# Batch 0's v pieces issued by ScalarE, small constants by SyncE, and a later gate for the first weight load

## The chip, the core and the metric

The kernel runs on one core of a Trainium2 chip. The core has a matrix engine (TensorE, PE in the profile), a vector engine (VectorE, DVE), an engine for activation functions (ScalarE, ACT), a general engine (GpSimd, POOL) and SyncE (SP), which here only issues DMAs. Sixteen DMA engines move the data. SyncE, ScalarE and GpSimd each have a DMA queue of their own. The metric is the device time of one execution in microseconds, and lower is better.

## What is computed

The reference is linear attention without a softmax, then an RMS norm per head, then a gated convolutional feed-forward block. Inputs are float32: q, k, v of 8 batches x 8 heads x 576 positions x 64, w_in 512 x 1024, conv_w 3 x 1024, w_out 1024 x 512.

```python
kv  = einsum('bhsd,bhse->bhde', k, v)            # 64 x 64 per head
o   = einsum('bhsd,bhde->bhse', q, kv)
o   = o / sqrt(mean(o * o, axis=-1) + 1e-6) * g_norm
x   = o.transpose(0, 2, 1, 3).reshape(8, 576, 512)
h   = maximum(x @ w_in, 0)
c   = sum over 3 taps of conv_w[tap] * h shifted by tap - 1 along the sequence
out = (h * sigmoid(c)) @ w_out                   # 8 x 576 x 512
```

## The kernel before, in words

The whole program is one list, `ORDER` (lines 59 to 122). Each word of it names a small function and its arguments; a number behind an @ chooses a buffer or PSUM bank. The words are run from left to right, and at the end each instruction is tied to the one before it on its engine, so every engine works through its instructions in exactly the order of the list. An engine that waits holds back everything that stands behind it.

Heads are put in pairs: 128 partitions hold two heads of 64, so each of q, k and v of a batch is four column blocks (t = 0 to 3). Positions are kept as 64 partitions x 9 rows. Batches 1 to 7 are loaded by GpSimd, which turns float32 into bfloat16 on the way (`Lq`, `Lk`, `Lv`, line 321). So are the weights: `Li` (line 335) brings w_in in two halves, `Lo` (line 339) w_out. Batch 0 goes another way. `pre` (lines 226 to 250) has SyncE load it as float32 in twelve pieces, in the order of `HEAD` (line 218): q.t.s is two blocks and part of the columns (256 KB for q.0.0 and q.1.0, 320 KB for q.0.1 and q.1.1), k.t and v.t are one block each (288 KB). `cad` casts a piece to bfloat16 on VectorE (line 358), `caa` on ScalarE (line 360).

The small constants (three rows of convolution taps and the norm's weights, `cw_rows`) are loaded by ScalarE (lines 237 and 238). `ct` (line 268) transposes them on TensorE; `pc` (lines 274 to 281) has VectorE copy them out of PSUM and rescale them, in eight small instructions.

The part of the list that counts here is its head. On TensorE it is: `fi.78.64`, 78 matmuls on zeros whose results nobody reads; `ct`; `qt.0.0.0`, transposes of q; `fi.17.512`, 17 more matmuls on zeros; `kv.0.0.1`, the k-v products of the first four heads; then `fi.1`, `qt`, `ot`, `fi.3`, `oq`, `fi.8` and `kv.0.1.1`, the products of the other four heads. These `fi` words keep TensorE busy at the start (line 263). On VectorE it is: cast of q.0.0, `pl` (memsets), `pc`, casts of k.0, v.1, q.1.0 and k.2, `ps` (lines 300 to 305), cast of v.3, `qd` (line 417), `dg.7`, `kvd.0.1.1` (line 388), `dg.4`, cast of q.0.1 and so on. On ScalarE: casts of v.0 and k.1, `qa`, `kva`, `sq`, casts of v.2 and k.3, `nl`. The head ends with `hp` (line 555), the first matmuls with w_in; from there on it is mostly long runs of matmuls.

`gt` (line 352) is the gate of the weight load. It copies one column of a staged piece on GpSimd, and since GpSimd works in order, w_in and all later loads of that queue are issued only when that piece has arrived. Here the piece is q.1.0.

DMAs issued by SyncE and ScalarE report their arrival on eight semaphores, which the framework gives out in rotation over both engines. A DMA that gets a semaphore whose earlier user has not yet arrived waits for it before it is issued. In this kernel the ninth to fourteenth of the loads, k.2, v.2, k.3, v.3, q.0.1 and q.1.1, have such waits, on the constants' taps, q.0.0, the norm's weights, k.0, v.0 and k.1.

Of the kernel before, what the change touches and what calls it, by code (L numbers as in the profile page):

```python
# [56 lines left out]


ORDER = """
pre@0,1 af gt.q.1.0 Li.0.4 fi.78.64@0 ct@0 cad.q.0.0@0 caa.v.0.0@0 pl pc cad.k.0.0@0 caa.k.1.0 cad.v.1.0 cad.q.1.0  # L60
cad.k.2.0 ps cad.v.3.0 qt.0.0.0@2 fi.17.512@1 qa.0.0.0@0 kv.0.0.1@4 kva.0.0.1@0 fi.1.512@0 qt.0.1.0@6 qd.0.1.0@1
Li.4.4 ot.0.0.0@2 sq.0.0.0@0 dg.7 fi.3.512@0 oq.0.0.0@4 fi.8.512@0 caa.v.2.0 caa.k.3.0 kv.0.1.1@0 fi.2.512@6 kvd.0.1.1
ot.0.1.0@6 fi.2.512@0 dg.4 nl.0.0.0@0 sq.0.1.0@1 cad.q.0.1 qt.0.0.1@4 qa.0.0.1 mo.0.0.0@0 cad.q.1.1 oq.0.1.0@0
# [62 lines left out]
def kernel(  # L126
# [11 lines left out]
    nc = tc.nc  # L138
    B, H, S, D = q.shape
    D_model = H * D  # L140
    D_ff = moe_w_in.shape[1]
    P = 128
# [5 lines left out]
    NF = D_ff // P  # L148
# [11 lines left out]
    def ring(r, shape, dtype, name):  # L160
        return work.tile(shape, dtype, name=name, tag=f"{r}{slots.pop(0)}", bufs=1)


    def half(i):
        return slice(i * D, (i + 1) * D)
# [4 lines left out]
    def heads(x, b, t0, n):  # L170
        return src[x][b, 2 * t0:2 * (t0 + n)].rearrange("(t i) (p r) d -> (i p) t (r d)", i=2, r=R)

    T = {}
# [7 lines left out]
    NR = 3 * NF + 1  # L181
# [3 lines left out]
    cw_rows = consts.tile([NR, P], FP32, name="cw_rows")  # L185
    cw = consts.tile([P, NR], FP32, name="cw")
# [24 lines left out]
    def act_table(which):  # L211
        if act_set[0] != which:
            act_set[0] = which
            nc.scalar.preload_act_table_set(  # L214
                {"rs": "abs_reciprocal_sqrt_and_small", "sig": "sigmoid_and_others"}[which])

    RS = ((0, 4), (4, 9))
    HEAD = "q.0.0 k.0.0 v.0.0 k.1.0 v.1.0 q.1.0 k.2.0 v.2.0 k.3.0 v.3.0 q.0.1 q.1.1"

    def cols(b, s):  # L220
        if b == 0:
            return tuple(r * D for r in RS[s])
        return s * HS, (s + 1) * HS

    @op
    def pre():
        T["stg"] = ring("h", [P, 2, NT, R * D], FP32, "stg")
        T["stq"] = ring("h", [P, NT, R * D], FP32, "stq")
        for what in HEAD.split():
            x, t, s = what.split(".")  # L230
            t, s = int(t), int(s)
            if x == "q":
                ts, (c0, c1) = slice(2 * t, 2 * t + 2), cols(0, s)
                nc.sync.dma_start(out=T["stq"][:, ts, c0:c1], in_=heads("q", 0, 2 * t, 2)[:, :, c0:c1])
            else:
                nc.sync.dma_start(out=T["stg"][:, "kv".index(x), t:t + 1, :], in_=heads(x, 0, t, 1))  # L236
        nc.scalar.dma_start(out=cw_rows[:3 * NF, :], in_=moe_conv_w.rearrange("k (f p) -> (k f) p", p=P))
        nc.scalar.dma_start(
            out=cw_rows[NR - 1:NR, :].rearrange("o (i d) -> o i d", i=2),
            in_=g_norm.unsqueeze(0).unsqueeze(1).to_broadcast([1, 2, D]))  # L240
        act_table("rs")
        nc.vector.memset(zero, 0.0)  # L242
        nc.vector.memset(ident, 0.0)
        nc.vector.memset(ones, 0.0)
        for i in range(2):
            nc.vector.memset(ones[half(i), half(i)], 1.0)
        nc.vector.memset(eps_sb, eps)
        for t in taps:
            nc.vector.memset(t[:, 0, :, :, 7:8], 0.0)
            nc.vector.memset(t[:, 1, :, :, S:S + 1], 0.0)  # L250
# [425 lines left out]
    for token in ORDER.split():  # L676
        what, _, at = token.partition("@")
# [44 lines left out]
```

## Time and profile before

| | |
|---|---|
| median of 3 runs | 187.1 us (186.58 to 187.44) |
| the profiled execution | 186.68 us, of which the span from first to last instruction is 184.9 us |
| TensorE busy | 174.6 us, 94% of the span |
| VectorE, ScalarE, GpSimd busy | 145.7, 147.9 and 19.2 us |
| first matmul with w_in (line 555) | 19.73 us after the start |

Times in the rows are microseconds from the start of the span. In a timeline row stand the start, the length, the engine, the line, the operation, what it writes and reads, and, in square brackets, how long the engine sat idle before it and what ended that. An engine name with a q (SPq, ACTq, POOLq) is an instruction that issues a DMA; its length is the issuing alone, and the data arrive later. The chain of waits is followed backwards from the last instruction, at each step to what released it.

### The profile page before, as it was taken

How to read it: one execution, taken by the hardware profiler on the slowest of the kernel's cores; microseconds unless marked ns; L12 is line 12 of the kernel's file. 1: busy time of each engine (PE TensorE's matmuls, PEld its weight loads, DVE VectorE, ACT ScalarE, POOL GpSimd, SP SyncE). 2: the span in 40 equal slices, each digit the busy share in tenths (PEclk: the TensorE clock that was granted, in tenths of full speed). 3: DMA queues.
4: the chain of work that ended last, by engine and by line, in shares of the span. 5: the costliest groups of instructions: out<-in, count | busy, mean ns of one | idle time of the engine just before them, and what ended most of it. 6: DMA issues, size and time to landing. Idle time of an engine off the chain costs nothing.

```text
span 184.9 us, 5517 instructions
## 1 busy us (share of the span) xinstructions
PE 174.6 (94%) x2358; PEld 107.5 (58%) x2358; DVE 145.7 (79%) x283; ACT 147.9 (80%) x232; POOL 19.2 (10%) x30
## 2 busy tenths in 40 slices
PE   7998899999989899999999999999999999999990
PEld 7543677645657587447567784454578754444450
DVE  3578701864589979999599999997999999999650
ACT  2456789877788999999999997999979977673830
POOL 1095200300413001600000000000000000000000
PEclk9999999999999999999999999999999999999997
DMA  5999999999999996899940000102320001417294
GB/s 176 289 345 200 206 210 205 209 208 255 231 208 208 208 209 103 131 208 221 278 97 4 4 0 4 57 20 97 130 100 0 0 0 57 174 51 289 80 380 167
DMA packets 20816, 27.82 MB, mean 150 GB/s; under 512 B 1184, under 2 KB 15288, under 8 KB 20792
## 3 DMA queue, kind: packets, MB, share of 16 engines
q0 software_dynamic: 13184, 14.48, 46.7%
q1 hardware_dynamic: 7568, 12.98, 20.0%
q8 instruction: 18, 0.29, 0.6%
q14 instruction: 6, 0.05, 0.1%
q10 hardware_dynamic: 40, 0.01, 0.0%
HBM read 32.52 MB, written 9.44 MB: 227 GB/s over the span
## 4 chain that ended last, share of the span: by engine, by line
PE 73%; DVE 13%; DMA 4%; ACT 3%; issue 2%; SPq 2%; DVEq 0%; ACTq 0%
PE banks L629 30%; PE banks L540 24%; PE banks L555 4%; DMA stg<-in_v_dram 4%; PE banks L605 3%; DVE qT L417 3%; PE banks L434 2%; PE banks L376 2%; PE banks L407 2%; SPq L236 2%; DVE x L526 2%; DVE h L619 1%; DVE taps L579 1%; ACT rs L472 1%; DVE taps L578 1%
## 5 line engine op out<-in xcount | busy, mean ns | idle before, releaser
L629 PE MATMUL banks<-w_out_sb,h 128*128 128x512 bf16 x280 | 64.2, 380 | 0.3 <-DVE row L640 0.3
L540 PE MATMUL banks<-x,w_in_sb 128*128 128x288 bf16 x448 | 57.6, 286 | 0.7 <-DVE x L526 0.2
L540 PEld LDWEIGHTS <-w_in_sb 128*128 128x128 bf16 x448 | 43.2, 98 | 13.6 <-issue 1.6
L629 PEld LDWEIGHTS <-h 128*128 128x128 bf16 x280 | 26.3, 98 | 31.3 <-issue 2.5
L595 ACT ACTIVATE taps<-taps,cw 128x576 bf16<-128x576 bf16 (+1 forms) x40 | 37.3, 967 | 7.8 <-DVE taps L589 7.8
L546 ACT ACTIVATE h<-banks 128x576 bf16<-128x576 f32 x56 | 34.2, 658 | 2.7 <-PE banks L540 2.7
L619 DVE TENSOR_TENSOR h<-h,taps 128x1152 bf16<-128x1152 bf16 (+1 forms) x24 | 22.8, 953 | 11.8 <-ACT taps L612 10.1
L442 ACT ACTIVATE sq<-banks 128x576 bf16<-128x576 f32 (+2 forms) x32 | 20.4, 660 | 4.4 <-PE banks L434 4.1
L584 DVE TENSOR_TENSOR taps<-taps 128x1152 bf16<-128x1152 bf16 (+1 forms) x20 | 20.0, 999 | 0.4
L589 DVE TENSOR_TENSOR taps<-taps,h 128x1152 bf16<-128x1152 bf16 (+1 forms) x20 | 19.8, 996 | 0.5
L578 DVE TENSOR_SCALAR taps<-h,cw 128x576 bf16<-128x576 bf16 (+1 forms) x40 | 17.2, 429 | 1.1 <-ACT h L546 1.1
L579 DVE TENSOR_SCALAR taps<-h,cw 128x576 bf16<-128x576 bf16 (+1 forms) x40 | 17.4, 436 | 0.0
L635 ACT ACTIVATE row<-banks 128x512 f32<-128x512 f32 x26 | 14.9, 600 | 2.9 <-PE banks L629 2.5
L483 DVE SCALAR_TENSOR_TENSOR x<-banks,cw,rs 128x576 bf16<-128x576 f32 (+2 forms) x16 | 12.9, 814 | 4.9 <-ACT rs L472 4.8
L263 PE MATMUL banks<-zero 128*128 128x64 bf16 (+1 forms) x113 | 12.9, 282 | 1.2 <-DVE zero L242 1.2
L526 DVE SCALAR_TENSOR_TENSOR x<-o,cw,banks 128x576 bf16<-128x576 f32 x16 | 12.2, 810 | 2.1 <-PE banks L520 2.1
L472 ACT ACTIVATE rs<-banks,eps_sb 128x576 f32<-128x576 f32 (+2 forms) x16 | 11.6, 738 | 1.2 <-PE banks L455 1.1
L417 DVE COPY qT<-banks 128x1152 bf16<-128x1152 bf16 (+2 forms) x15 | 10.4, 712 | 2.3 <-PE banks L407 1.5
L214 ACT ACT_TABLE_LOAD x8 | 10.3, 1283 | 2.3 <-issue 2.2
L448 ACT ACTIVATE o<-banks 128x576 f32<-128x576 f32 x16 | 10.4, 675 | 0.3 <-PE banks L434 0.3
L321 POOL DMA_DIRECT2D k_sb<-in_k_dram x7 | 5.3, 755 | 45.0 <-PE banks L376 44.4
L434 PE MATMUL banks<-qT,kvb 64*64 64x288 bf16 (+2 forms) x128 | 8.6, 296 | 1.3 <-DVE qT L417 0.9
(78 smaller groups left out, 143.1 us busy)
## 6 DMA issues: line engine op xcount, KB each, us to landing
out_dram<-row SPq DMA_DIRECT2D x35, 256.0 KB, 2.4
q_sb<-in_q_dram POOLq DMA_DIRECT2D x7, 576.0 KB, 17.9
k_sb<-in_k_dram POOLq DMA_DIRECT2D x7, 576.0 KB, 13.6
v_sb<-in_v_dram POOLq DMA_DIRECT2D x7, 576.0 KB, 15.6
stg<-in_k_dram SPq DMA_DIRECT2D x4, 288.0 KB, 4.0
stg<-in_v_dram SPq DMA_DIRECT2D x4, 288.0 KB, 6.4
w_in_sb<-in_moe_w_in_dram POOLq DMA_DIRECT2D x2, 512.0 KB, 8.6
w_out_sb<-in_moe_w_out_dram POOLq DMA_DIRECT2D x1, 1024.0 KB, 20.0
```

What stands on the lines that cost most here:

```text
L417: nc.vector.tensor_copy(to, fr)
L442: nc.scalar.activation(T["sq", b, u, s], T["o", b, u, s], AX.Square)
L526: nc.vector.scalar_tensor_tensor(x_part(b, u, s), T["o32", b, u, s], g_sb, T["sp", b, u, s], op0=AL.mult, op1=AL.mult)
L540: nc.tensor.matmul(ps[:, s, :c1 - c0], w_in_sb[:, t, f * P:(f + 1) * P], T["x", b][:, t, c0:c1], start=(t == 0), stop=(t == NT - 1))
L546: nc.scalar.activation(h_of(b, f), T["hm", b, f][:, :, :HS].rearrange("p e (r n) -> p e n r", r=R), AX.Relu)
L578: nc.vector.tensor_scalar_mul(tap[:, 0, f % 2, :n, 8:8 + S], h[:, f], cw[:, f:f + 1])
L579: nc.vector.tensor_scalar_mul(tap[:, 1, f % 2, :n, :S], h[:, f], cw[:, 2 * NF + f:2 * NF + f + 1])
L584: nc.vector.tensor_add(tap[:, 1, :, :n, :S], tap[:, 0, :, :n, 7:7 + S], tap[:, 1, :, :n, 1:1 + S])
L589: nc.vector.tensor_add(y, y, span(b, n)[:, 2 * j:2 * j + 2])
L595: nc.scalar.activation(y, y, AX.Sigmoid, scale=cw[:, NF + f:NF + f + 1])
L619: nc.vector.tensor_mul(h, h, tap_of(b, j)[:, 1, :, :n, :S])
L629: nc.tensor.matmul(T["om", p, m], h[:, f, m * P:(m + 1) * P], w_out_sb[:, f, :], start=(f == 0), stop=(f == NF - 1))
```

## The change

Batch 0's four pieces of v are issued by ScalarE, one behind the other, as its first instructions. SyncE issues q, k and the small constants: q.0.0, k.0, k.1, then the two constant loads, then q.1.0, k.2, k.3, q.0.1, q.1.1. The gate of w_in reads a column of k.2 in place of q.1.0. Nothing else of the list is touched; all engines but SyncE and ScalarE keep their instructions and their order.

The rotation of the eight semaphores falls differently. By the compiled instruction lists, these DMAs of SyncE now wait before they are issued: the norm's weights (second constant load) for v.0, q.1.0 for q.0.0, k.2 for k.0, k.3 for v.1, q.0.1 for k.1, q.1.1 for v.2. The four v pieces and the load of the taps wait for nothing.

```diff
 ORDER = """
-pre@0,1 af gt.q.1.0 Li.0.4 fi.78.64@0 ct@0 cad.q.0.0@0 caa.v.0.0@0 pl pc cad.k.0.0@0 caa.k.1.0 cad.v.1.0 cad.q.1.0
+pre@0,1 af gt.k.2.0 Li.0.4 fi.78.64@0 ct@0 cad.q.0.0@0 caa.v.0.0@0 pl pc cad.k.0.0@0 caa.k.1.0 cad.v.1.0 cad.q.1.0
...
-    HEAD = "q.0.0 k.0.0 v.0.0 k.1.0 v.1.0 q.1.0 k.2.0 v.2.0 k.3.0 v.3.0 q.0.1 q.1.1"
+    HEAD = (("sync", "q.0.0 k.0.0 k.1.0 cw q.1.0 k.2.0 k.3.0 q.0.1 q.1.1"),
+            ("scalar", "v.0.0 v.1.0 v.2.0 v.3.0"))
...
-        for what in HEAD.split():
-            x, t, s = what.split(".")
-            ...
-                nc.sync.dma_start(out=T["stq"][:, ts, c0:c1], in_=heads("q", 0, 2 * t, 2)[:, :, c0:c1])
-            else:
-                nc.sync.dma_start(out=T["stg"][:, "kv".index(x), t:t + 1, :], in_=heads(x, 0, t, 1))
-        nc.scalar.dma_start(out=cw_rows[:3 * NF, :], in_=moe_conv_w.rearrange("k (f p) -> (k f) p", p=P))
-        nc.scalar.dma_start(
-            out=cw_rows[NR - 1:NR, :].rearrange("o (i d) -> o i d", i=2),
-            in_=g_norm.unsqueeze(0).unsqueeze(1).to_broadcast([1, 2, D]))
+        for name, head in HEAD:
+            queue = getattr(nc, name)
+            for what in head.split():
+                if what == "cw":
+                    queue.dma_start(out=cw_rows[:3 * NF, :], in_=moe_conv_w.rearrange("k (f p) -> (k f) p", p=P))
+                    queue.dma_start(
+                        out=cw_rows[NR - 1:NR, :].rearrange("o (i d) -> o i d", i=2),
+                        in_=g_norm.unsqueeze(0).unsqueeze(1).to_broadcast([1, 2, D]))
+                    continue
+                x, t, s = what.split(".")
+                ...
+                    queue.dma_start(out=T["stq"][:, ts, c0:c1], in_=heads("q", 0, 2 * t, 2)[:, :, c0:c1])
+                else:
+                    queue.dma_start(out=T["stg"][:, "kv".index(x), t:t + 1, :], in_=heads(x, 0, t, 1))
```

More of the change, by code (lines that the diff above doesn't have):

```diff
@@ L228, in pre @@
         T["stq"] = ring("h", [P, NT, R * D], FP32, "stq")
-        for what in HEAD.split():
-            x, t, s = what.split(".")
[L231 to L234, printed above, removed]
-            else:
-                nc.sync.dma_start(out=T["stg"][:, "kv".index(x), t:t + 1, :], in_=heads(x, 0, t, 1))
-        nc.scalar.dma_start(out=cw_rows[:3 * NF, :], in_=moe_conv_w.rearrange("k (f p) -> (k f) p", p=P))
-        nc.scalar.dma_start(
-            out=cw_rows[NR - 1:NR, :].rearrange("o (i d) -> o i d", i=2),
-            in_=g_norm.unsqueeze(0).unsqueeze(1).to_broadcast([1, 2, D]))
+        for name, head in HEAD:
[8 more added lines that the diff above has]
+                x, t, s = what.split(".")
+                t, s = int(t), int(s)
+                if x == "q":
+                    ts, (c0, c1) = slice(2 * t, 2 * t + 2), cols(0, s)
+                    queue.dma_start(out=T["stq"][:, ts, c0:c1], in_=heads("q", 0, 2 * t, 2)[:, :, c0:c1])
+                else:
+                    queue.dma_start(out=T["stg"][:, "kv".index(x), t:t + 1, :], in_=heads(x, 0, t, 1))
         act_table("rs")
```

## The prediction

> **What bounds the kernel now.** I read the page's busy shares and chain first, then the chain in order of time, then the first 20 us as a timeline.
>
> ```profile
> PE 174.6 (94%) x2358; PEld 107.5 (58%) x2358; DVE 145.7 (79%) x283; ACT 147.9 (80%) x232; POOL 19.2 (10%) x30
> PE 73%; DVE 13%; DMA 4%; ACT 3%; issue 2%; SPq 2%; DVEq 0%; ACTq 0%
> ```
>
> TensorE is the bound nearly throughout: a microsecond by which the head gets longer has no idle time behind it to vanish in. The chain in order of time shows the head:
>
> ```profile
> 5.62 7.80 DMA stg<-in_v_dram
> ...
> 13.45 0.53 DVE v_sb L358
> ...
> 14.63 0.21 DVE kvb L388
> ...
> 19.73 4.41 PE banks L555 x36
> ```
>
> It starts with SyncE's issues and the landing of the last v piece, then goes over VectorE's casts to the first matmul with w_in at 19.73. So v looks late. The timeline shows what stands just beside that chain:
>
> ```profile
> 0.74 0.43 SPq L234 DMA_DIRECT2D stq<-in_q_dram  x1
> 0.74 0.65 ACTq L237 DMA_DIRECT2D cw_rows<-in_moe_conv_w_dram  x1
> 1.43 0.70 ACTq L238 DMA_DIRECT2D cw_rows<-in_g_norm_dram  x1
> 2.16 1.28 ACT L214 ACT_TABLE_LOAD   x1 [2.16 <-issue]
> 3.67 0.43 DVE L358 CAST q_sb<-stq 128x512 bf16<-128x512 f32 x1 [1.81 <-DMA stq<-in_q_dram]
> 5.29 0.24 PE L268 MATMUL banks<-ident,cw_rows 25*128 25x25 f32 x1
> 5.71 3.84 PE L263 MATMUL banks<-zero 128*128 128x512 bf16 x17
> 6.05 0.68 ACT L360 ACTIVATE v_sb<-stg 128x576 bf16<-128x576 f32 x1 [2.61 <-DMA stg<-in_v_dram]
> 6.28 1.70 SPq L234 DMA_DIRECT2D stq<-in_q_dram  x2
> 8.31 0.46 DVE L358 CAST v_sb<-stg 128x576 bf16<-128x576 f32 x1 [0.86 <-DMA stg<-in_v_dram]
> 9.22 0.43 DVE L358 CAST q_sb<-stq 128x512 bf16<-128x512 f32 x1 [0.45 <-DMA stq<-in_q_dram]
> 9.25 0.44 POOL L352 COPY gate<-stq 128x1 f32<-128x1 f32 x1 [7.68 <-DMA stq<-in_q_dram]
> 9.48 0.48 PE L376 MATMUL banks<-v_sb,k_sb 64*64 64x64 bf16 x36
> 9.63 1.84 POOL L335 DMA_DIRECT2D w_in_sb<-in_moe_w_in_dram  x2
> 9.97 0.46 DVE L358 CAST k_sb<-stg 128x576 bf16<-128x576 f32 x1 [0.32 <-DMA stg<-in_k_dram]
> 11.70 1.90 PE L263 MATMUL banks<-zero 128*128 128x512 bf16 x8
> 12.66 0.68 ACT L360 ACTIVATE k_sb<-stg 128x576 bf16<-128x576 f32 x1
> 13.45 0.53 DVE L358 CAST v_sb<-stg 128x576 bf16<-128x576 f32 x1 [0.24 <-DMA stg<-in_v_dram]
> 13.53 0.22 PE L376 MATMUL banks<-v_sb,k_sb 64*64 64x64 bf16 x2
> 14.03 0.47 PE L376 MATMUL banks<-v_sb,k_sb 64*64 64x64 bf16 x34 [0.29 <-DVE v_sb L358]
> 14.55 0.29 DVE L388 CAST kvb<-banks 128x128 bf16<-128x128 f32 x1
> ```
>
> TensorE is full from the transpose of the constants (`ct`, 5.29) to `kv.0.1.1` (13.53): the 17 and the 8 zero matmuls stand in its order whether the data are there or not. Its second k-v group waits for v.3 by only 0.29 us. So two paths of almost equal length meet there: v.3 through VectorE, and `ct` plus the zero matmuls through TensorE. Speeding up the first wins next to nothing; delaying the second costs in full.
>
> **The change, part by part.**
>
> *The v pieces on ScalarE.* The DMA engines, and not the issuing, pace the head:
>
> ```profile
> 2.00:3.00 1.00, 1.00 (x24) 1.00 (x21) 0.00 (x0) 0.84 (x1) 0.00 (x0) 1.00 0.94 264
> 8.00:9.00 1.00, 1.00 (x7) 0.43 (x5) 0.46 (x1) 0.37 (x1) 0.00 (x0) 1.00 1.00 294
> ```
>
> In these stretches (the last two columns are the DMA share and GB/s) the engines are 94 to 100% busy, while SyncE has issued its last piece at 6.28 + 1.70 = 7.98. A second issuer moves the same 3,456 KB in another order. v.3 comes some microseconds earlier, and that is worth the 0.29 us wait plus what VectorE loses through it: with v.3 there, kv.0.1.1 would end near 13.53 + 0.47 = 14.0 and the copy `kvb` start there and not at 14.55, so 0.5 us at most. ScalarE issues four DMAs in place of two: 4 x 0.70 = 2.8 from 0.74, then the table load of 1.28, ready at 4.8, inside its 2.61 us idle before 6.05. Cost nothing; without that cover it would be about 1.4.
>
> *The constants on SyncE.* This is the part that costs. The taps now stand behind q.0.0, k.0 and k.1 in SyncE's queue, 256 + 288 + 288 = 832 KB, and the v pieces flow beside them. The norm's weights also wait until v.0 has landed before they are issued, and SyncE's later pieces stand behind that wait. `ct` needs both. Behind `ct` wait, on TensorE, `qt.0.0.0`, the 17 zero matmuls and all the rest; on VectorE, `pc` and every cast but the first. When do they land? With the queues sharing evenly, 2 x 832 = 1,664 KB go first. In the kernel before, 1,408 KB were in when v.1 was cast (8.31, idle until the DMA) and 1,664 KB when q.1.0 was (9.22). The taps touch 24 partitions only and need not wait for the slowest share, so I take 8.4, close to the first of the two. Bounds: v.0 can be in no earlier than q.0.0 is now (3.67), plus an issue of 0.70 is 4.4; if the load were instant and the taps overtook, `ct` would keep its 5.29 and the cost is nothing. The late end is the row of k.2, 9.97. So `ct` moves by +3.1 (0 to +4.7). From there to kv.0.1.1 TensorE has no idle time to give back, so that end moves by 3.1 and gains back the 0.5 above: **+2.6 us**. VectorE keeps up: its later casts lose the 0.86 + 0.45 + 0.32 of waiting that they had.
>
> The Trainium skill, "DMA: Bandwidth & Descriptors", section "Queues, rings and completion order", says that each DMA engine takes descriptors of one ring in order and goes round-robin between rings, by packets. The first half agrees with the order in which the pieces are cast here; by the second, were a packet one row, the 512 rows ahead of the taps (q.0.0 has 256 short ones) would let all 512 rows of v pass, 1,984 KB, just past k.2's 9.97, and the sum would be +4.2 in place of +2.6.
>
> *TensorE's clock.* The 78 zero matmuls end at about 5.3, and now nothing follows until 8.4: some 3.1 us of idling that the trace of before does not have in its head. The only such pause is at the end of the run, where the last matmul ends at 179.87:
>
> ```profile
> L263 PEld LDWEIGHTS <-zero x71: 102/132/132, 1.2 to 4.9; 128*128 128x128 bf16 x71
> ```
> ```profile
> L263 PEld LDWEIGHTS <-zero x7: 98/98/132, 4.9 to 5.1; 128*128 128x128 bf16 x7
> ```
> ```profile
> 179.00:180.00 1.00, 0.87 (x8) 0.53 (x6) 0.42 (x1) 0.04 (x1) 0.00 (x0) 1.00 1.02 381
> 182.00:183.00 1.00, 0.00 (x0) 0.00 (x0) 0.00 (x0) 0.00 (x0) 0.00 (x0) 0.75 0.39 133
> 183.00:184.90 1.90, 0.00 (x0) 0.00 (x0) 0.00 (x0) 0.00 (x0) 0.00 (x0) 0.50 0.02 6
> ```
>
> The granted clock (seventh column) averages 0.75 from 182 to 183 and 0.50 after, so it fell to half at 182.5, 2.6 us after the last matmul. At the start the zero matmuls' weight loads shorten from 132 to 98 ns (middle numbers) at about 5.0, 3.8 us after the first one at 1.2: there the clock came up, just before they end. If the clock falls in the new pause and needs 3.8 us again, half of that, 1.9 us, is lost, under the 17 zero matmuls. Bounds: nothing (no fall), and another 3.84 if all 17 run at half speed. Whether a pause of 3.1 us trips it depends on a phase that no row gives; 2.6 did once. I take the middle of nothing and 1.9, **+1.0 us**.
>
> *The later gate.* k.2 has 256 + 3 x 288 + 256 = 1,376 KB up to its own end on SyncE's queue and the four v pieces beside it, 2,528 KB; that is k.3's place before, cast at 12.66 right behind another cast. I take 12.0 (9.97 to 12.66), against the gate's 9.25: w_in is issued 2.75 us later.
>
> The first row is that of w_in's two DMAs, the second the first use of w_in in the timeline.
>
> ```profile
> DMA to landing us min/median/max: 7.8/8.6/9.4
> ```
> ```profile
> 19.43 0.10 PEld L555 LDWEIGHTS <-w_in_sb 128*128 128x128 bf16 x1 [0.25 <-issue]
> ```
>
> The halves landed at 9.63 + 7.8 = 17.4 and about 20.1; they would at 20.2 and 22.9 in the worst case. Their first users move from 19.43 to 23.0, and the second half is used some 2 us later still. Hidden, with 2 us to spare. GpSimd's later loads move with it, by less than their users do. Without that cover (head not delayed) 0.8 us would show. VectorE's cast of k.2 moves too: 12.0 - 9.97 = 2.0, less the 0.24 of waiting for v.3, puts `kvb` at 16.3; TensorE delivers kv.0.1.1 at 14.0 + 3.1 = 17.1, so that hides as well.
>
> **The sum.** 186.68 (the profiled execution: 184.9 of span and 1.8 around it) + 2.6 + 1.0 = 190.3. The median of the runs shown is 0.4 above the profiled one; half of that on top gives **190.5 us**.
>
> **The rivals.**
>
> *The clock does not fall.* The pause of 3.1 us passes, and the 17 zero matmuls keep their 3.84 us: 186.68 + 2.6 + 0.2 = 189.5. For it speaks that the phase is open, against it the 2.6 us that sufficed at the end of the trace. Chance 0.24. The Trainium skill, "TensorE: Matmul & The Clock Gate", Part 1, says that the clock drops after at least one idle window of about 3.4 us; by that rule the pause would pass, and the time be this one.
>
> *The constants come in time, and k.2 is late instead.* If a short load slips past the pieces, `ct` stays near 5.3 to 6.5 and VectorE's wait for k.2 replaces the wait for v.3: 16.3 against 14.55, +1.8, so 188.5 (187.0 if k.2 comes at 10.4). For it speaks that ScalarE's two constant loads were in by 5.29 with pieces already flowing; against it, that they had a queue to themselves. Chance 0.14.
>
> *Not slower.* The two queues together draw more than one, and everything is earlier: then v.3's wait goes, -0.5, 186.4. The point of decision is `ct`: at 5.5 or earlier, with k.2 in by about 10.2, this holds. For it: the stretch from 3 to 4 us ran faster than that from 8 to 9.
>
> ```profile
> 3.00:4.00 1.00, 1.00 (x23) 1.00 (x21) 0.33 (x1) 0.44 (x1) 0.00 (x0) 1.00 0.94 344
> ```
>
> Against it: at 344 GB/s from 2.0 on, the 1,664 KB (1.70 MB) still end at 7.0. Chance 0.1, and even then the gain stays below 0.5%, save in the best case.
>
> **How the numbers follow.** Main case (constants late, clock partly lost, 189.6 to 192.8) 0.52, clock kept 0.24, k.2 late 0.14, not slower 0.10. The range 188.0 to 192.8 holds the first two nearly whole and half of the third. A difference of 0.5%, 0.9 us here, is about the spread of the three runs, and less can't be told from none. Slower by more: 0.52 + 0.24 + two thirds of 0.14 + a little = 0.86; within: 0.11; faster by more: 0.03.
>
> **What would show it.** In the new profile: the transpose at line 273 near 8.4 with TensorE idle before it and a DMA as the releaser; the 17 zero matmuls right behind, longer than 3.84 us if the clock fell (weight loads of 132 ns in place of 98, a PEclk below 9 in slices 1 to 3); VectorE's copy of the constants waiting some 3 us; the first matmul with w_in near 23; the rest of the run as long as before. I am wrong if the transpose starts before 6.5, or if the first matmul with w_in comes later but the end does not.

## The result and the profile after

The changed kernel takes 191.8 us (median of 4 runs, 191.02 to 192.21) against 186.85 us (median of 4, 186.58 to 187.44) for the kernel before: a ratio of 1.0256, 95% interval 1.0208 to 1.0303. It is slower by 4.95 us. The profiled execution took 192.18 us with a span of 190.3. Ratios, here and below, leave out runs that were over 1.5% above the fastest of their kernel. From line 219 on the changed kernel has other line numbers: the transpose of the constants is line 273, the zero matmuls are 268, the k-v products 381, the gate 357, the loads of w_in 340, the first matmuls with w_in 560.

The chain of the changed kernel in order of time (start, length, what):

```profile
0.73 3.39 DMA stg<-in_v_dram
...
4.14 4.30 DMA cw_rows<-in_g_norm_dram
...
9.17 5.90 PE banks L268 x17
...
17.28 1.83 PE banks L268 x8
...
24.80 1.25 PE banks L560 x10
```

The chain before went over SyncE's issues, the last piece of v and VectorE's casts. Now it goes from v.0 to the norm's weights, whose issue waits for it, and from there through TensorE's own list, the zero matmuls included. The timeline of the changed kernel:

```profile
0.73 1.88 ACTq L245 DMA_DIRECT2D stg<-in_v_dram  x4
2.22 0.52 SPq L234 DMA_DIRECT2D cw_rows<-in_moe_conv_w_dram  x1
4.14 0.69 SPq L235 DMA_DIRECT2D cw_rows<-in_g_norm_dram  x1
...
7.97 0.68 ACT L365 ACTIVATE k_sb<-stg 128x576 bf16<-128x576 f32 x1 [3.13 <-DMA stg<-in_k_dram]
...
8.54 0.27 PE L273 MATMUL banks<-ident,cw_rows 25*128 25x25 f32 x1 [3.01 <-DMA cw_rows<-in_g_norm_dram]
8.85 0.19 DVE L279 COPY cw<-banks 128x25 f32<-128x25 f32 x1 [2.83 <-PE banks L273]
9.10 5.97 PE L268 MATMUL banks<-zero 128*128 128x512 bf16 x17
9.92 0.18 POOL L357 COPY gate<-stg 128x1 f32<-128x1 f32 x1 [8.35 <-DMA stg<-in_k_dram]
10.04 1.88 POOL L340 DMA_DIRECT2D w_in_sb<-in_moe_w_in_dram  x2
...
15.00 0.48 PE L381 MATMUL banks<-v_sb,k_sb 64*64 64x64 bf16 x36
...
19.05 0.48 PE L381 MATMUL banks<-v_sb,k_sb 64*64 64x64 bf16 x36
19.59 0.29 DVE L393 CAST kvb<-banks 128x128 bf16<-128x128 f32 x1 [2.73 <-PE banks L381]
```

The transpose moves from 5.29 to 8.54, the 17 zero matmuls behind it from 5.71 to 9.10 (+3.39). They take 5.97 us in place of 3.84 (+2.13). The second half of the first product no longer waits for v.3, it runs in one block, which gives 0.48 back: `kvb` stands at 19.59 against 14.55, +5.04 = 3.39 + 2.13 - 0.48. The first matmul with w_in follows at 24.80 against 19.73 (+5.07).

All of it is in the head. Busy time by stretches, first before, then after (length, busy time of PE, PEld, DVE, ACT and POOL with counts, granted clock, DMA share, GB/s):

```profile
20.00:184.90 164.90, 157.15 (x2067) 97.33 (x2065) 132.54 (x218) 137.66 (x217) 11.13 (x15) 0.99 0.64 139
3.00:10.00 7.00, 7.00 (x119) 4.62 (x116) 3.59 (x22) 2.29 (x4) 0.75 (x2) 1.00 0.98 308
```
```profile
25.07:190.30 165.23, 157.14 (x2067) 97.33 (x2065) 132.50 (x218) 137.60 (x217) 10.39 (x14) 0.99 0.60 132
3.00:10.00 7.00, 3.99 (x68) 3.20 (x66) 1.97 (x16) 2.89 (x4) 0.08 (x1) 1.00 1.06 390
```

From the first matmuls with w_in on, TensorE has the same 2067 matmuls and the same 157.1 us of work; the stretch is 0.33 us longer. In the head (3 to 10 us) TensorE is busy 3.0 us less, while the DMA engines moved 390 GB/s in place of 308.

### The profile page after: what moved, and what is told of

Read it like the earlier page. It is cut to its first block, busy times and chain, and to the rows that moved or that the text cites. A ratio compares the mean times of both kernels' runs of the same rounds, so it can differ in the third digit from the quotient of the medians.

```text
span 190.3 us, 5515 instructions
## 1 busy us (share of the span) xinstructions
PE 176.9 (93%) x2358; PEld 108.2 (57%) x2358; DVE 146.1 (77%) x283; ACT 147.7 (78%) x232; POOL 19.2 (10%) x30
## 4 chain that ended last, share of the span: by engine, by line
PE 74%; DVE 14%; DMA 4%; ACT 3%; issue 2%; DVEq 0%; ACTq 0%
PE banks L634 29%; PE banks L545 22%; PE banks L268 5%; PE banks L560 4%; PE banks L610 3%; DVE qT L422 3%; PE banks L381 2%; PE banks L412 2%; DMA cw_rows<-in_g_norm_dram 2%; PE banks L439 2%; DMA stg<-in_v_dram 2%; DVE x L531 2%; DVE x L488 2%; DVE taps L584 2%; DVE taps L583 1%
## 5 line engine op out<-in xcount | busy, mean ns | idle before, releaser
L268 PE MATMUL banks<-zero 128*128 128x64 bf16 (+1 forms) x113 | 15.2, 308 | 1.2 <-DVE zero L247 1.2
L268 PEld LDWEIGHTS <-zero 128*128 128x128 bf16 x113 | 7.7, 126 | 6.1 <-issue 3.1
```

The lines of the kernel that those rows point to most:

```text
L268: nc.tensor.matmul(ps[:, :w], zero[:, :P], zero[:, :w], start=True, stop=True)
```

## The experiments

The theory at the outset was that the constants' place in SyncE's queue makes the loss, and the clock a part of it. The rivals were v's move itself, the later gate, and the wait of the norm's weights for v.0. `HEAD` is the list of issues by engine, `ORDER` the list of the program; the diffs are against the changed kernel, where nothing else is said.

### Constants back on ScalarE, ahead of v

```diff
-    HEAD = (("sync", "q.0.0 k.0.0 k.1.0 cw q.1.0 k.2.0 k.3.0 q.0.1 q.1.1"),
-            ("scalar", "v.0.0 v.1.0 v.2.0 v.3.0"))
+    HEAD = (("sync", "q.0.0 k.0.0 k.1.0 q.1.0 k.2.0 k.3.0 q.0.1 q.1.1"),
+            ("scalar", "cw v.0.0 v.1.0 v.2.0 v.3.0"))
```

> The changed kernel with one part undone: the two constant loads are ScalarE's first DMAs again, ahead of the v pieces; q and k stay on SyncE, the gate stays on k.2. Theory (the constants' queue place is the whole loss): they land before the 78 zero matmuls end, the transpose of the constants runs at about 5.3, the first matmul with w_in at 19.2 to 19.8, 186.4 to 187.2 us. Rival (v on ScalarE, or the later gate, costs by itself): it stays above 188.5 us with the transpose at 5.3.

Measured: 188.18 us (187.88 to 189.43), ratio 1.0072 (1.0040 to 1.0103). Timeline of this kernel:

```profile
5.47 0.30 PE L273 MATMUL banks<-ident,cw_rows 25*128 25x25 f32 x1
...
8.91 0.68 ACT L365 ACTIVATE v_sb<-stg 128x576 bf16<-128x576 f32 x1 [2.90 <-DMA stg<-in_v_dram]
...
12.33 0.46 DVE L363 CAST k_sb<-stg 128x576 bf16<-128x576 f32 x1 [1.08 <-DMA stg<-in_k_dram]
...
15.80 0.47 PE L381 MATMUL banks<-v_sb,k_sb 64*64 64x64 bf16 x34 [0.97 <-DVE v_sb L363]
```

Three quarters of the loss are gone with the constants in time. What stays is a new one: v.0 lands 2.9 us later than before (cast at 8.91 against 6.05) although it was issued at 2.17, and k.2 delays the cast of v.3. The time lies between the two expectations, and neither named v.0.

### Constants alone moved, v left on SyncE

Against the kernel before: the two constant loads go to SyncE behind k.1, and nothing else is changed.

```diff
-    HEAD = "q.0.0 k.0.0 v.0.0 k.1.0 v.1.0 q.1.0 k.2.0 v.2.0 k.3.0 v.3.0 q.0.1 q.1.1"
+    HEAD = (("sync", "q.0.0 k.0.0 v.0.0 k.1.0 cw v.1.0 q.1.0 k.2.0 v.2.0 k.3.0 v.3.0 q.0.1 q.1.1"),
+            ("scalar", ""))
```

> The kernel before with one part of the change alone: the constants are issued by SyncE behind k.1, everything else (v on SyncE, gate on q.1.0) as before. They stand behind 1,120 KB on one queue. Theory (queue place): the transpose runs at 7.2 to 7.6, when k.1 is in, and the kernel takes 188.5 to 191 us, the upper part if the 17 zero matmuls run at half speed. Rival (two queues side by side are needed for the loss): the transpose near 5.3 and 187 us.

Measured: 189.82 us (187.73 to 191.22), ratio 1.0093 (1.0045 to 1.0142). The runs fall in two groups, 187.7 to 187.8 and 189.5 to 191.2. Timeline:

```profile
7.15 0.27 PE L273 MATMUL banks<-ident,cw_rows 25*128 25x25 f32 x1 [1.61 <-DMA cw_rows<-in_moe_conv_w_dram]
...
8.11 4.81 PE L268 MATMUL banks<-zero 128*128 128x512 bf16 x16 [0.33 <-issue]
```

The constants' place costs by itself, without v's move: the transpose is 1.86 us late, and the zero matmuls behind it are slow here too. The upper group lies in the range of the theory (188.5 to 191 us) or just above it, the lower one 0.8 us above the kernel before.

### Constants first on SyncE

```diff
-    HEAD = (("sync", "q.0.0 k.0.0 k.1.0 cw q.1.0 k.2.0 k.3.0 q.0.1 q.1.1"),
+    HEAD = (("sync", "cw q.0.0 k.0.0 k.1.0 q.1.0 k.2.0 k.3.0 q.0.1 q.1.1"),
```

> The changed kernel with the constants as SyncE's first two DMAs, ahead of q.0.0. Theory (place in the queue, not the engine that issues): the transpose at about 5.3 as before; q and k come about 1 us later than in the changed kernel since two issues of 0.5 to 0.7 stand ahead of them; 186.4 to 187.6 us. Rival (SyncE as issuer of these small loads is the cause): above 189 us.

Measured: 192.18 us (191.46 to 193.53), ratio 1.0273 (1.0202 to 1.0344): as slow as the change. Timeline, then the packets of the two queues from 3 to 4 us (q10 is ScalarE's, q1 SyncE's; packets, MB, share of the DMA engines):

```profile
1.96 0.42 SPq L243 DMA_DIRECT2D stq<-in_q_dram  x1
...
5.46 0.30 PE L273 MATMUL banks<-ident,cw_rows 25*128 25x25 f32 x1
...
8.77 0.43 DVE L363 CAST q_sb<-stq 128x512 bf16<-128x512 f32 x1 [6.91 <-DMA stq<-in_q_dram]
...
10.01 4.87 PE L268 MATMUL banks<-zero 128*128 128x512 bf16 x16 [0.33 <-issue]
```
```profile
q10 hardware_dynamic: 168, 0.33, 103.9%
q1 hardware_dynamic: 5, 0.00, 1.0%
```

The transpose is on time, as expected, and that is worth nothing: q.0.0, which is issued at 1.96 behind the constants, arrives only for a cast at 8.77 (3.67 before). Its transposes stand between `ct` and the zero matmuls on TensorE, so it takes the constants' place. The time is the rival's (above 189 us), but not for the rival's reason: SyncE as the issuer did not make the constants late. From 3 to 4 us v fills the DMA engines and SyncE's queue moves next to nothing, in good part because q.0.0 has only started: its first packets go at 3.89, 1.9 us after its issue (1.1 us in the kernel before, 1.7 in the changed one). From 4 to 7 us SyncE's queue has 55, 109 and 125 packets a microsecond beside ScalarE's 72, 83 and 86. So v on ScalarE is not free where something needed early is issued after it.

### Constants one place further up

```diff
-    HEAD = (("sync", "q.0.0 k.0.0 k.1.0 cw q.1.0 k.2.0 k.3.0 q.0.1 q.1.1"),
+    HEAD = (("sync", "q.0.0 cw k.0.0 k.1.0 q.1.0 k.2.0 k.3.0 q.0.1 q.1.1"),
```

> The changed kernel with the constants one place up in SyncE's queue, behind q.0.0 and ahead of k.0. By the compiled list k.1 now waits for v.0 before it is issued. Theory, as the earlier runs have changed it (whatever SyncE issues after ScalarE's v pieces comes after them, and the first late one of the pieces that TensorE or VectorE meet in their order sets the head): the transpose at about 5.4, but k.1 lands at 8.5 to 10, so the first k-v products start at 10 to 11.5 in place of 9.48, and the kernel takes 187.5 to 189.5 us. Rival (only the place of the constants counts): 186.5 to 187.3 us.

Measured: 187.42 us (187.19 to 189.22), ratio 1.0044 (1.0007 to 1.0080). Timeline, and the packets of the two queues from 4 to 5 us:

```profile
6.03 0.21 PE L273 MATMUL banks<-ident,cw_rows 25*128 25x25 f32 x1 [0.52 <-DMA cw_rows<-in_g_norm_dram]
...
6.42 3.84 PE L268 MATMUL banks<-zero 128*128 128x512 bf16 x17
...
9.54 0.68 ACT L365 ACTIVATE k_sb<-stg 128x576 bf16<-128x576 f32 x1 [4.32 <-DMA stg<-in_k_dram]
...
10.19 0.56 PE L381 MATMUL banks<-v_sb,k_sb 64*64 64x64 bf16 x36
```
```profile
q10 hardware_dynamic: 171, 0.35, 95.3%
q1 hardware_dynamic: 7, 0.00, 1.3%
```

This is the cleanest test: v stays on ScalarE, the gate stays on k.2, and two small loads change places with two pieces of k. It gives back 4.4 of the 4.95 us (191.8 - 187.42), the clock's share included; the time lies just under the range of the theory and just above that of the rival. The transpose waits 0.52 us in place of 3.01, and the zero matmuls are at full speed. k.0 and k.1 are now the late ones, since again SyncE's queue moved almost nothing for a while behind the constants, but here the zero matmuls cover that.

### The norm's weights without their wait for v.0

v.3 goes to SyncE behind the constants. The constants keep their place, but the semaphores fall so that the norm's weights are issued without a wait.

```diff
-    HEAD = (("sync", "q.0.0 k.0.0 k.1.0 cw q.1.0 k.2.0 k.3.0 q.0.1 q.1.1"),
-            ("scalar", "v.0.0 v.1.0 v.2.0 v.3.0"))
+    HEAD = (("sync", "q.0.0 k.0.0 k.1.0 cw v.3.0 q.1.0 k.2.0 k.3.0 q.0.1 q.1.1"),
+            ("scalar", "v.0.0 v.1.0 v.2.0"))
```

> The changed kernel with the fourth piece of v moved to SyncE's queue behind the taps, so that ScalarE issues three pieces. The constants keep their place behind q.0.0, k.0.0 and k.1.0, but the norm's weights no longer wait for v.0's landing before they are issued. Theory (the place in the queue sets the constants): the transpose still at 7.5 to 8.6, and 190.0 to 192.0. Rival (the wait for v.0 ahead of the issue set them): the transpose at 5.5 to 6.8, and 187.0 to 189.0.

Measured: 191.75 us (191.13 to 192.21), ratio 1.0266 (1.0223 to 1.0308). Timeline:

```profile
2.72 0.69 SPq L235 DMA_DIRECT2D cw_rows<-in_g_norm_dram  x1
...
7.64 0.68 ACT L365 ACTIVATE k_sb<-stg 128x576 bf16<-128x576 f32 x1 [2.92 <-DMA stg<-in_k_dram]
...
7.89 0.27 PE L273 MATMUL banks<-ident,cw_rows 25*128 25x25 f32 x1 [2.36 <-DMA cw_rows<-in_moe_conv_w_dram]
```

The norm's weights are issued at 2.72 in place of 4.14, and the transpose still starts at 7.89, 0.25 us behind the cast of k.1, now held up by the taps. So some 2.6 of the 3.25 us are the place in the queue, and the wait for v.0 explains at most about 0.65; ScalarE's queue is a piece shorter here, so the split is not exact. The theory's expectation held.

### A longer run of zeros at the start

To take the pause on TensorE away, `fi.78` becomes `fi.190`: the zeros last until the constants are there.

```diff
-pre@0,1 af gt.k.2.0 Li.0.4 fi.78.64@0 ct@0 ...
+pre@0,1 af gt.k.2.0 Li.0.4 fi.190.64@0 ct@0 ...
```

> The changed kernel with 190 short zero matmuls ahead of the transpose in place of 78, so that TensorE does not idle while it waits for the constants. Nothing else changes; the constants still land near 8.4. Theory (the clock is one of two terms): the 17 long zero matmuls behind take 3.8 us in place of 5.97, and the kernel 189.7 to 190.3 us, 1.5 to 2 less than the changed one. Rival (the long zero run in the trace is a symptom that does not set the end): 191.5 to 192 us, as the changed kernel.

Measured: 190.59 us (189.99 to 190.85; the profiled execution 189.99), ratio 1.0185 (1.0117 to 1.0252). Timeline:

```profile
8.60 0.24 PE L273 MATMUL banks<-ident,cw_rows 25*128 25x25 f32 x1
...
9.24 3.62 PE L268 MATMUL banks<-zero 128*128 128x512 bf16 x16 [0.16 <-issue]
...
22.59 2.58 PE L560 MATMUL banks<-x,w_in_sb 128*128 128x256 bf16 x21 [0.23 <-ACT rs L477]
```

The transpose starts as late as with the change (8.60), but the zero matmuls are back at full speed, and the first matmul with w_in starts 2.21 us earlier than with the change (22.59 against 24.80). So the clock is a loss of its own: 2.2 us between the two profiled executions (192.18 - 189.99), 1.2 us between the medians. The four runs (189.99 to 190.85) all lie below the four of the change (191.02 to 192.21); the median is 0.3 us above the range of the theory.

### The gate alone

Against the kernel before:

```diff
-pre@0,1 af gt.q.1.0 Li.0.4 ...
+pre@0,1 af gt.k.2.0 Li.0.4 ...
```

> The kernel before with the gate alone moved from q.1.0 to k.2. Theory: w_in is issued 0.7 to 0.8 us later (k.2's cast at 9.97 against q.1.0's 9.22), its halves land 0 to 0.8 us later, still before their first use, and the time is that of the kernel before within 0.5%, 186.5 to 187.5 us. Rival (w_in is on the edge): 187.5 to 188.

Measured: 187.39 us (186.31 to 189.12), ratio 1.0027 (0.9988 to 1.0066): no difference that can be told from none.

### Constants on GpSimd's queue

```diff
-    HEAD = (("sync", "q.0.0 k.0.0 k.1.0 cw q.1.0 k.2.0 k.3.0 q.0.1 q.1.1"),
+    HEAD = (("gpsimd", "cw"),
+            ("sync", "q.0.0 k.0.0 k.1.0 q.1.0 k.2.0 k.3.0 q.0.1 q.1.1"),
```

> The changed kernel with the constants issued by GpSimd, as its first DMAs, so that neither SyncE's nor ScalarE's queue has them; q, k and v are issued as in the changed kernel. Theory: the constants are in by 5.3 and the pieces land as in the changed kernel (k.1 near 8, k.2 near 9.9, k.3 near 10.6), so nothing of the head is late: 186.2 to 187.2 us, the time of the kernel before, because the zero matmuls set the head then. Rival (v on ScalarE costs by itself, as 188.18 us with the constants on ScalarE might say): 188 us or more.

Measured: 191.45 us (189.4 to 193.16), ratio 1.0202 (1.0109 to 1.0296). Timeline (lines one higher here):

```profile
1.27 0.67 POOL L235 DMA_DIRECT2D cw_rows<-in_moe_conv_w_dram  x1 [0.83 <-POOLq L712]
1.93 0.54 POOL L236 DMA_DIRECT2D cw_rows<-in_g_norm_dram  x1
...
8.87 0.27 PE L274 MATMUL banks<-ident,cw_rows 25*128 25x25 f32 x1 [3.93 <-DMA cw_rows<-in_g_norm_dram]
```

A queue with nothing ahead of them does not help: issued at 1.27 and 1.93, they release the transpose at 8.87. The theory's expectation failed outright; the rival's number (188 us or more) came out, but not by its cause, as the constants were late. Small loads can also be late on a queue of their own, when two others keep the DMA engines full. In the trace GpSimd's queue has its first packet at 4.88, 3.6 us after the issue, 62 of its 64 packets between 4 and 7 us, and the last between 8 and 9. What holds them there this case does not show.

A second kernel had the same, with shorter zero runs and v.3 cast ahead of the spread build:

```diff
-cad.k.2.0 ps cad.v.3.0 qt.0.0.0@2 fi.17.512@1 ...
+cad.k.2.0 cad.v.3.0 ps qt.0.0.0@2 fi.13.512@1 ...
-... oq.0.0.0@4 fi.8.512@0 ...
+... oq.0.0.0@4 fi.3.512@0 ...
```

> The kernel with the constants on GpSimd and a head cut to the new landing times: 13 long zero matmuls in place of 17, 3 in place of 8 ahead of the second k-v products, and VectorE's cast of v.3 ahead of the eleven small additions and not behind them. Theory: with all pieces in by about 10.6 (k.3) the second k-v products start near 12 in place of 13.5 and w_in still comes in time; 185.0 to 186.2 us, less than either kernel. Rival (another wait takes over, w_in or the casts): 186.5 to 187.5.

Measured: 190.15 us (189.5 to 190.84), ratio 1.0170 (1.0101 to 1.0239). The transpose stood at 7.54, and 13 zero matmuls took 4.67 us: late constants and a slow clock again, and a time above both expectations.

### Three tries at a faster head

The first takes the kernel with the constants one place further up, casts v.3 ahead of the spread build, and cuts 8 zero matmuls to 4.

```diff
-cad.k.2.0 ps cad.v.3.0 qt.0.0.0@2 fi.17.512@1 ...
+cad.k.2.0 cad.v.3.0 ps qt.0.0.0@2 fi.17.512@1 ...
-... oq.0.0.0@4 fi.8.512@0 ...
+... oq.0.0.0@4 fi.4.512@0 ...
```

> The changed kernel with the taps one place further up (behind q.0.0 alone), and two cuts in the head: the last piece of v is cast ahead of the spread build, which held up the second half of the first product in the run with the taps one place further up, and 4 zero matmuls stand in place of 8. Theory (the constants' place was the loss, and with it gone the head ends with the last casts): the transpose near 6.0, the second part of the first product begins 1 to 1.5 us earlier than in that run, the first product of the hidden layer near 18.8 to 19.5, and the time 186.0 to 187.0. Rival (the last pieces land too late for the casts' order to matter, or the shorter stretch of zeros costs clock): no earlier than 20.0, 187.3 to 188.5.

Measured: 188.98 us (187.12 to 190.35), ratio 1.0081 (1.0046 to 1.0116), in two groups: 5 of 12 runs at 187.1 to 187.5, 7 at 188.9 to 190.4. The profiled execution is of the upper group. Timeline:

```profile
6.02 0.27 PE L273 MATMUL banks<-ident,cw_rows 25*128 25x25 f32 x1 [0.48 <-DMA cw_rows<-in_g_norm_dram]
...
6.58 5.66 PE L268 MATMUL banks<-zero 128*128 128x512 bf16 x17
```

The constants are as early as in the kernel that it is made from, but the same 17 zero matmuls take 1.82 us more (5.66 against 3.84). The groups lie about 2 us apart, much the same amount. The lower group stands where most runs of the parent stand (187.2 to 187.6), so the cut itself wins nothing; even that group is above the theory's range (186.0 to 187.0).

The second takes the kernel before and gives ScalarE only v.2 and v.3, behind the constants; the gate stays on q.1.0:

```diff
-    HEAD = "q.0.0 k.0.0 v.0.0 k.1.0 v.1.0 q.1.0 k.2.0 v.2.0 k.3.0 v.3.0 q.0.1 q.1.1"
+    HEAD = (("sync", "q.0.0 k.0.0 v.0.0 k.1.0 v.1.0 q.1.0 k.2.0 k.3.0 q.0.1 q.1.1"),
+            ("scalar", "cw v.2.0 v.3.0"))
```

> The kernel before, with v.2 and v.3 alone moved to ScalarE, where they stand behind the two constant loads; the constants stay first on ScalarE, the other pieces stay on SyncE in their order, and the gate stays on q.1.0. Theory (a second queue draws more from the DMA engines, and what loses is only what stands behind a late piece or behind the norm's weights): the transpose stays at 5.2 to 5.6, no wait for v.3 at the second half of the first product, and 186.0 to 186.8, no slower than before. Rival (v.2 and v.3 take the DMA engines' time from k.1, v.1 and q.1.0, which are needed sooner): v.1 cast at 9.0 or later, the first half of the first product at 10.0 or later in place of 9.48, and 187.2 to 188.5.

Measured: 187.99 us (187.69 to 188.69), ratio 1.0060 (1.0041 to 1.0079). Timeline:

```profile
9.88 0.46 DVE L363 CAST v_sb<-stg 128x576 bf16<-128x576 f32 x1 [2.19 <-DMA stg<-in_v_dram]
10.04 0.82 PE L381 MATMUL banks<-v_sb,k_sb 64*64 64x64 bf16 x36
```

With the constants in time (the transpose at 5.46), the gate as before and two pieces of v moved, it is still slower. v.1 is cast at 9.88 in place of 8.31: the late pieces on the second queue take DMA time from a piece that is needed sooner. The rival's numbers held. The third try adds shorter zero runs and the other order of casts to this one:

```diff
-cad.k.2.0 ps cad.v.3.0 qt.0.0.0@2 fi.17.512@1 ...
+cad.k.2.0 cad.v.3.0 ps qt.0.0.0@2 fi.15.512@1 ...
-... oq.0.0.0@4 fi.8.512@0 ...
+... oq.0.0.0@4 fi.4.512@0 ...
```

> The same as the kernel with only v.2 and v.3 on ScalarE, with 15 zero matmuls in place of 17 and 4 in place of 8, and v.3 cast ahead of the spread build. Theory: with the last pieces in earlier the zeros are what TensorE's order waits on, 6 x 0.226 = 1.4 us of them go, and the time is 185.0 to 186.0, faster than before. Rival (the first half is then bound by v.1's landing and the second by ScalarE's cast of k.3 at about 12.7): at most half a microsecond is won, 186.2 to 187.2.

Measured: 190.23 us (188.75 to 191.19), ratio 1.0157 (1.0119 to 1.0195). The first half of the product waits 1.81 us for v.1's cast and starts its main part at 11.01. The clock falls behind that wait: the trace's record of the granted clock has it at half from 11.70 to 15.11, and the next three zero matmuls take 1.46 us in place of 0.82. Both expectations were for a shorter time. No version that was run beats the kernel before.

## Why the prediction was right, and where it was off

The forecast was 190.5 (188.0 to 192.8), slower with 0.86; the medians say 191.8. The main case is the one that happened. By its steps:

**Two paths of equal length.** Right. Speeding up v won 0.48 us, of the 0.5 at most that was allowed; the delay of `ct` came through in full.

**v on ScalarE costs nothing.** Right for this kernel, with a wrong reason. "A second issuer moves the same 3,456 KB in another order" misses the pace: 390 GB/s in place of 308. And the other order is not harmless: with the constants earlier it still costs 0.7 and 1.2 us at the medians (187.42 against 186.75, where the transpose is itself 0.74 us late, and 188.18 against 186.96), and v.1 delayed by two pieces on the other queue costs 1.1 (187.99 against 186.91). In the change itself, late constants hide that.

**The constants on SyncE, +2.6.** Right in size: +3.25 at the transpose (3.1 forecast), +3.39 at the zero matmuls, less 0.48, is +2.9. That it came so close is luck: the working had two errors that cancel. It took 1,664 KB (1.70 MB) ahead of the taps; more went ahead, 2.02 MB by 7.5 us (269 GB/s from 0 on), when the last packets of the constants go, at a higher pace. Part of that pace could be seen before the change: up to 8.31 us the engines had moved 1.87 MB (225 GB/s), while the working counted only the pieces that were complete by then, 1,408 KB or 1.44 MB. Packets of the changed kernel from 7 to 8 us, then from 8 to 9:

```profile
q1 hardware_dynamic: 196, 0.17, 52.9%
q10 hardware_dynamic: 100, 0.19, 52.8%
```
```profile
q1 hardware_dynamic: 245, 0.38, 109.6%
```

ScalarE's queue is in motion until 8 us and gone after: all four pieces of v went ahead of, or beside, the taps. The Trainium skill, "DMA: Bandwidth & Descriptors", section "Queues, rings and completion order", has the rings served in turn by packets; by its rule, with a packet taken as one row, an estimate of 1,984 KB (2.03 MB) goes first, and this trace agrees with that volume (2.02 MB by 7.5 us). What made the sum by that rule too long (+4.2) was the pace of the kernel before, at which it was worked out. The turns are not always even, though: with the constants one place further up, 7 packets of SyncE's queue stood against 171 of ScalarE's from 4 to 5 us, and no run settles why.

**The clock, +1.0.** This is the step that failed in size, and in its story. Measured: +2.13. The step said "if the clock falls in the new pause". In the profiled execution it had not come up. The zero matmuls by tile, after, from 6 to 16 us, and before; then the weight loads, after, from 1 to 6 us and from 6 to 16 us:

```profile
L268 PE MATMUL banks<-zero x18: 379/622/634, 9.1 to 15.4; 128*128 128x512 bf16 x18
```
```profile
L263 PE MATMUL banks<-zero x33: 379/379/390, 5.7 to 15.4; 128*128 128x512 bf16 x33
```
```profile
L268 PEld LDWEIGHTS <-zero x78: 104/132/132, 1.2 to 5.2; 128*128 128x128 bf16 x78
...
L268 PEld LDWEIGHTS <-zero x18: 95/152/152, 9.1 to 15.4; 128*128 128x128 bf16 x18
```

None of the 78 first weight loads is down at 98 ns, where those of the kernel before were from 4.9 us on. So the 4.3 us of zeros ended, at 5.5, with the clock still down, the pause came, and ten of the 17 ran at 610 to 634 ns in place of 379. In the trace's record of the granted clock the first rise is at 5.01 us before and at 13.45 after. The longer run of zeros shows it: without the pause, no loss. (In its trace the clock rose at 5.12 already, so it shows a pause avoided, not a late rise mended.) The Trainium skill, "TensorE: Matmul & The Clock Gate", Part 1, says that the clock rises after a busy window of about 3.4 us and that the window runs freely, whatever the kernel does. The records agree on the window: within a run, changes lie 3.41 us apart or whole multiples of it (with the constants first on SyncE at 5.71, 9.12 and 12.53), at a phase that differs from run to run. How full a window has to be they leave open: with the gate alone the clock rose at 4.02, only 2.83 us after the first zero matmul, and in the first try at a faster head it did not rise at 6.89, behind a window with 2.94 us of matmuls. A busy stretch of 4.3 us then fills a window well enough at some phases and not at others. That would explain the two groups of runs; it is argued, as only one run of each kernel has a trace.

**The later gate.** Hidden, as said, but k.2 was mis-sized: in for the gate at 9.92, not 12.0, through the higher pace. w_in was issued at 10.04, 0.41 us later than before. The kernel with the gate alone shows no cost that can be told from none.

**The sum.** For the profiled execution 190.3 was forecast and 192.18 measured. Of the 1.9 between them the clock makes 1.1, the constants 0.3, and the longer stretch at the end 0.33: ScalarE's last copy is 5.06 us later than before (185.02 against 179.96), so that third lies behind the computing.

**The rivals.** "The clock does not fall" was answered by another question than the one asked, as the clock of the profiled execution had not risen. In three other traces it did rise and then fell in a pause of the head: at 5.71 and 9.12 with the constants first on SyncE, at 4.09 and 7.51 with them on GpSimd, at 4.79 and 8.20 with them there and shorter zero runs. Between rise and fall stood 0.05, 0.85 and 1.12 us of matmuls, so in the last two less than the wholly idle window that the prediction cites beside this rival was enough. What the step had in mind thus happens; which of the two a run meets would depend on the phase. "The constants come in time, and k.2 is late instead" did not happen in the change, but the kernel with the constants back on ScalarE is that case, forecast at 188.5 and measured at 188.18 (k.2 cast at 12.33 and `kvb` at 16.32, for 12.0 and 16.3 forecast). "Not slower" set its point at a transpose by 5.5 us and k.2 by 10.2; the kernels that moved pieces of v and had the transpose at about 5.5 were still 0.6 to 2.7% slower, but none of them had k.2 in by 10.2, so that point itself was not reached.

**The signs.** The transpose near 8.4 with a DMA as its releaser, the copy of the constants waiting some 3 us, the long zero matmuls and the unchanged rest all showed. The first matmul with w_in was forecast near 23 and came at 24.80, for the most part through the clock. Two signs were badly chosen: weight loads went to 152 ns and not 132, and the page's clock row shows 9 in every slice of the head, as the record only begins with the first rise.

## What to carry to other kernels

A small load that an in-order engine needs early should not stand behind bulk pieces, on its own queue or beside another that is full; its bytes do not count, what goes ahead of it does. A second DMA queue moves more, but it divides the engines between pieces needed now and later, where one queue in order of need does not. A stretch of filler that ends close to the clock's rise can be worth nothing if a pause follows: see where the weight loads get shorter, and how far from the end of the filler that is.

## What the runs showed of the hardware that was not expected

- Two queues issued by SyncE and ScalarE moved 390 GB/s from 3 to 10 us, one moved 308, with the DMA share at 1.06 and 0.98. In the other traces one queue moved 289 to 315, two 325 to 392. A full DMA share is not the top pace.
- A piece that follows the two small loads on its queue, beside a second queue that is full, came late. With the constants one place up, SyncE's queue moved 7 packets from 4 to 5 us and ScalarE's 171; k.0, issued at 2.46, had its first packet at 5.41. With the constants first on SyncE it was q.0.0, issued at 1.96, first packet at 3.89, cast at 8.77; with them first on ScalarE it was v.0, issued at 2.17 and cast at 8.91. Whether the small load itself holds the queue or the other queue's pieces crowd it out was not separated. With the constants on SyncE alone and no second queue, their packets passed from 5.3 to 6.5 us and the queue kept 321, 294 and 251 GB/s from 5 to 8 us, which speaks against the first.
- GpSimd's queue gave 12.5 KB no faster passage: 6.9 us from the issue of the norm's weights at 1.93 to the transpose that waited for them.
- TensorE's clock changed in steps of 3.41 us at a phase that differs by run, and filler of 4.3 us did not always raise it. It fell in pauses too, after a window that still held up to 1.60 us of matmuls in 3.41 (8.29 to 11.70, in the third try at a faster head).
